# A fused adaLN, cached-attention and gated-MLP decode step: the whole kernel rewritten around one load ring and transposed keys

## The chip, the cores and the metric

The kernel runs on one NeuronCore of a Trainium2 chip. The core has TensorE (PE; its weight loads are listed as PEld), VectorE (DVE), ScalarE (ACT), GpSimd (POOL) and SyncE (SP); 16 DMA engines move data between HBM and the on-chip SBUF, and TensorE writes its results to PSUM. The metric is device time in microseconds (us) of one execution. Before the change the median of three runs is 456.72 us (456.42 to 456.93).

A TensorE matmul needs two instructions: a weight load (LDWEIGHTS) that puts a tile of up to 128 x 128 into the array, and the MATMUL, which streams the other operand's columns through it and sums over the partitions. "A pair" below is one of each.

## The reference

One decode step of a transformer block for 8 sequences, hidden size 1024, in bf16:

```python
def reference(A_x, A_k_cache, A_v_cache, A_wq, A_wo, B_x, B_W_gate, B_W_up, B_W_down, c, w_mod):
    # attention: B=8, Sq=1, D=1024, Hq=32, Hkv=4, Sk=8192, Dh=128
        q = (x @ wq).reshape(B, Sq, Hq, Dh) ...
        k = jnp.repeat(k_cache, rep, axis=1)          # 8 query heads share a kv head
        scores = jnp.einsum('bhqd,bhkd->bhqk', q, k) * Dh ** (-0.5)
        p = _softmax(scores, axis=-1)
        o = jnp.einsum('bhqk,bhkd->bhqd', p, v)
        return ... o.reshape(B, Sq, Hq * Dh) @ wo
    # MLP: F=3584
        h = relu(x @ W_gate) * (x @ W_up);  return h @ W_down
    mod = (_silu(c) @ w_mod).reshape(8, 6, 1, -1)      # sa, ca, ga, sb, cb, gb
    h = _layernorm(x) * (1 + ca) + sa
    x = x + ga * attention(h)
    h = _layernorm(x) * (1 + cb) + sb
    x = x + gb * mlp(h)
```

Everything is read once: the K and V caches are 67 MB each, w_mod 12.6 MB, wq and wo 8.4 MB each, gate, up and down 7.3 MB each, 186 MB in all.

## The kernel before, in words

Activations are kept transposed: features on the 128 partitions, the 8 sequences in the columns. A weight tile of 128 x 128 is the stationary operand and an activation tile of 8 columns streams through it, so nearly every matmul has 8 columns.

The order of the work is written out per engine by a small planner. `gen_sp`, `gen_act`, `gen_dve` and `gen_pe` list each engine's instructions; a first dry run ranks TensorE's events, and the loads are sorted into the two queues by the rank of the event that frees their buffer. SP issues all weights and K, ACT issues V between its own work (all through line 61). Buffers are fixed: four weight slots (`wslot`), four K slots (`ksl`), three V slots (`vsl`), 16 KB per partition each, and a scratch area `scr`. Weights for the later stages go into K and V slots when these come free.

The stages:

- Start: c and x are loaded as rows, the sigmoid is taken (L305), silu and x are transposed on TensorE (L552, L556).
- Modulation: for each of eight 1.5 MB blocks of w_mod, 48 matmuls into one of two PSUM banks (L569), which DVE adds up in SBUF (L386). The first layernorm runs on 8-partition rows (function `layernorm`), and its result is transposed.
- Queries: four 2 MB blocks of wq, 64 matmuls each (L587), added up by DVE (L405); ACT scales and reorders them (L315).
- Attention, batch by batch: for each of the four kv heads 64 score matmuls (L508), whose stationary operand is a K tile as it lies in SBUF, positions on the partitions. DVE takes the maximum over all 2048 score columns of a batch (L410); two f32 matmuls and small DVE operations turn it into a bias on all partitions (L534, L413, L415, L537, L418); DVE subtracts it (L422), ACT takes the exponential (L324), DVE sums it (L427), two more f32 matmuls finish the sum (L542, L545). The 4 x 64 PV matmuls of a batch (L525) are issued in two halves during the next batch.
- After the last batch: 256 wo matmuls (L612), the residual, x1 turned to rows by f32 matmuls (L494), the second layernorm in rows, its transposition (L487).
- MLP: for each of eight blocks of gate and up 56 matmuls (L634), added up by DVE (L460); relu and product (L463); 224 down matmuls (L651) in four blocks; gate, residual, eight transposes of 128 columns (L660), a copy (L482) and the store.

A K slot is freed by its last score matmul, a V slot by its last PV matmul. The K tile goes into the score matmul like this:

```python
kv = T.ksl[:, kslot, :].rearrange("k (c d) -> k c d", d=Dh)
...
T.S_ps[:, col:col + REP], kv[:, cix, :], T.qT[:, b, REP * p:REP * (p + 1)],
```

Of the kernel before, what the change touches and what calls it, by code (L numbers as in the profile page):

```python
# [5 lines left out]
dt = mybir.dt  # L6
# [5 lines left out]
class _Eng:  # L12

    def __init__(self, K, name):
        self.K = K
        self.name = name
        self.count = 0
        self.e = None
        self.sem = None
        self.muted = True  # L20

    def _live(self):
        return self.K.emit and not self.muted

    def op(self, fn, key=None, sync=True):
        if sync:
            self.count += 1
        if self._live():
            ins = fn(self.e)
            if sync:  # L30
                ins.then_inc(self.sem, 1)
        if key is not None:
            self.mark(key)
        return self.count

    def mark(self, key):
        k = (self.name, key)
        if self.K.emit:
            assert self.K.ev[k] == self.count, (k, self.K.ev[k], self.count)
        else:  # L40
            assert k not in self.K.ev, k
            self.K.ev[k] = self.count

    def wait(self, eng_name, key):
        if self._live():
            val = self.K.ev[(eng_name, key)]
            self.e.wait_ge(self.K.engs[eng_name].sem, val)

    def wait_self(self):
        if self._live() and self.count > 0:  # L50
            self.e.wait_ge(self.sem, self.count)

    def wait_dma(self, sem_name, value):
        if self._live():
            self.e.wait_ge(self.K.dsem[sem_name], value)

    def dma(self, out_ap, in_ap, sem_name):
        c = self.K.dcnt.get(sem_name, 0) + 16
        self.K.dcnt[sem_name] = c
        if self._live():  # L60
            self.e.dma_start(out_ap, in_ap).then_inc(self.K.dsem[sem_name], 16)  # L61
        return c


class _K:
    pass


class _T:
    pass  # L70


DBG = {}


def bass_adaLN_cond__gqa_block_cached__glu_gated_reglu__decode_kernel(
# [20 lines left out]
    assert B == 8 and D == 1024 and Dh == 128 and Hq == 32 and G == 4 and REP == 8  # L97
    assert F % 128 == 0 and w_mod.shape[1] == 6 * D
    assert Sk % 128 == 0
    NCX = Sk // 128  # L100
    NCOL = NCX * G * REP
    assert NCOL <= 2048
    KC = D // 128
    NKC2 = F // 128
    inv_sqrt_dh = float(Dh) ** -0.5
    EPS = 1e-5
    NW = 4
    NV = 3
    NKT = 4

    K = _K()
    K.ev = {}
    K.emit = False
    K.dcnt = {}
    K.pe_rank = None
    K.engs = {nm: _Eng(K, nm) for nm in ("sp", "act", "pool", "dve", "pe")}

    wblocks = []
    for kc in range(KC):
        wblocks.append(("mod", kc, [(lambda r: r[:, 0:6 * D], w_mod[128 * kc:128 * (kc + 1), :])]))  # L120
    for jb in range(KC // 2):
        wblocks.append(("wq", jb, [(lambda r: r[:, 0:2 * HQD].rearrange("p (k n) -> p k n", n=HQD),
                                    A_wq[256 * jb:256 * (jb + 1), :].rearrange("(kc p) n -> p kc n", p=128))]))
    for blk in range(4):
        wblocks.append(("wo", blk, [(lambda r: r[:, 0:KC * 1024].rearrange("p (k n) -> p k n", n=1024),
                                     A_wo[1024 * blk:1024 * (blk + 1), :].rearrange("(hh d) n -> d hh n", d=128))]))
# [5 lines left out]
    while r0 < F:  # L132
        rr = min(1024, F - r0)
        wd_rows.append((r0, rr))
        r0 += rr
# [8 lines left out]
    for n in range(B * G):  # L144
        last_k_user[n % NKT] = n
# [626 lines left out]
```

## Time and profile before

| | |
|---|---|
| median of three runs | 456.72 us (456.42 to 456.93) |
| the profiled execution, first to last instruction | 453.9 us; the runs' median is 2.8 us above that span |
| busy time | PE 183.6 us, DVE 100.9, ACT 22.5, POOL 1.3 |
| moved by DMA | 186.40 MB, 411 GB/s over the span |
| score matmuls (L508) | 2048, 58.3 us busy |
| PV matmuls (L525) | 2048, 60.1 us busy |
| DVE passes over a batch's scores (L410, L422, L427) | 2292, 2291 and 3568 ns each, 8 of each |
| K and V loads | 32 of 2048 KB each, median 29.4 and 18.7 us from issue to landing |

The span is that of one profiled execution; the times are of other executions, and include what lies around the span. Busy time of an engine is the union of its instructions' times. The rows of 40 slices cut the span into stretches of 11.35 us. A group's line names the line of the kernel, engine, operation, output and inputs, shape and count, then busy us and the mean ns of one, then the idle time just before them and what ended it. Matmuls are pipelined, so the mean time of one (168 ns) is much longer than their distance in a stream.

### The profile page before, as it was taken

To read this page: it belongs to the slowest core of one execution; us is meant where nothing else is said; L and a number is where in the kernel's file an instruction comes from. 1 tells how busy PE (TensorE), PEld (TensorE's weight loads), DVE (VectorE), ACT (ScalarE), POOL (GpSimd) and SP (SyncE) were. 2 spreads that over 40 slices of the span, in tenths; PEclk is the share of its full clock that TensorE was granted. 3 is DMA by queue.
4 is the path that set the end of the run, shared out by engine and by line. 5 is a ranking of instruction groups with operands and counts; after the bars stand their busy time and mean duration, and the time that the engine had idled before them with its cause. 6 is when DMAs were issued, how large, how long until landed. Compare 5 with 4: busy or idle time off the path is not lost.

```text
span 453.9 us, 11940 instructions
## 1 busy us (share of the span) xinstructions
PE 183.6 (40%) x5784; PEld 170.6 (38%) x5784; DVE 100.9 (22%) x120; ACT 22.5 (5%) x16; POOL 1.3 (0%) x9
## 2 busy tenths in 40 slices
PE   1212433418445226072407240733073573364655
PEld 1212433307345226062406240633063462263655
DVE  5000200062322320043004300430043043003321
ACT  3000001010100100001000100100010011000000
POOL 1000000000000000000000000000000000000000
PEclk9999999999999999999999999999999999999555
DMA  7999999999999999999999999999999989999992
GB/s 309 431 431 426 422 435 428 429 430 372 427 429 424 435 422 425 422 433 422 430 423 430 431 416 430 430 428 419 436 424 432 394 357 428 420 423 424 414 405 77
DMA packets 21662, 186.40 MB, mean 411 GB/s; under 512 B 1624, under 2 KB 1624, under 8 KB 11376
## 3 DMA queue, kind: packets, MB, share of 16 engines
q1 hardware_dynamic: 17008, 118.54, 62.5%
q10 hardware_dynamic: 4608, 67.11, 34.8%
q8 instruction: 45, 0.74, 0.6%
q14 instruction: 1, 0.01, 0.0%
HBM read 185.63 MB, written 0.02 MB: 409 GB/s over the span
## 4 chain that ended last, share of the span: by engine, by line
DMA 65%; PE 19%; DVE 6%; issue 5%; another core or an unknown queue 3%; ACT 1%; SPq 1%
DMA ksl<-in_A_k_cache_dram 43%; DMA vsl<-in_A_v_cache_dram 12%; DMA wslot<-in_w_mod_dram 10%; PE S_ps L508 7%; PE OT_ps L525 4%; PE X_ps L612 2%; DVE guacc L427 2%; PE X_ps L634 1%; PE OT_ps L634 1%; DVE scr L422 1%; PE X_ps L651 1%; ACT scr L324 1%; PE S_ps L494 1%; SPq L61 1%
## 5 line engine op out<-in xcount | busy, mean ns | idle before, releaser
L525 PE MATMUL OT_ps<-scr,vsl 128*128 128x8 bf16 x2048 | 60.1, 168 | 87.5 <-DMA vsl<-in_A_v_cache_dram 76.7
L508 PE MATMUL S_ps<-qT,ksl 128*128 128x8 bf16 x2048 | 58.3, 168 | 89.5 <-DMA ksl<-in_A_k_cache_dram 76.5
L525 PEld LDWEIGHTS OT_ps<-scr,vsl 128*128 128x128 bf16 x2048 | 57.3, 104 | 89.8 <-DMA vsl<-in_A_v_cache_dram 77.8
L508 PEld LDWEIGHTS S_ps<-qT,ksl 128*128 128x128 bf16 x2048 | 56.5, 104 | 91.2 <-DMA ksl<-in_A_k_cache_dram 74.1
L410 DVE TENSOR_REDUCE guacc<-S_ps 128x32 f32<-128x2048 f32 x8 | 18.3, 2292 | 145.5 <-PE S_ps L508 145.5
L427 DVE TENSOR_REDUCE guacc<-scr 128x32 f32<-128x2048 bf16 x8 | 28.5, 3568 | 15.8 <-ACT scr L324 15.8
L324 ACT ACTIVATE scr<-scr 128x2048 bf16<-128x2048 f32 x8 | 15.3, 1909 | 286.4 <-DVE scr L422 286.4
L422 DVE TENSOR_TENSOR scr<-S_ps,guacc 128x2048 f32<-128x2048 f32 x8 | 18.3, 2291 | 0.3
L569 PE MATMUL X_ps<-siluT,wslot 128*128 128x8 bf16 x192 | 5.8, 168 | 17.4 <-DMA wslot<-in_w_mod_dram 17.4
L569 PE MATMUL OT_ps<-siluT,wslot 128*128 128x8 bf16 x192 | 5.8, 168 | 16.5 <-DMA wslot<-in_w_mod_dram 16.5
L569 PEld LDWEIGHTS X_ps<-siluT,wslot 128*128 128x128 bf16 x192 | 5.4, 104 | 17.7 <-DMA wslot<-in_w_mod_dram 15.0
L569 PEld LDWEIGHTS OT_ps<-siluT,wslot 128*128 128x128 bf16 x192 | 5.4, 104 | 16.8 <-DMA wslot<-in_w_mod_dram 16.8
L430 DVE RECIPROCAL guacc<-X_ps 1x32 f32<-1x32 f32 x8 | 2.8, 346 | 37.5 <-PE X_ps L542 37.5
L612 PE MATMUL X_ps<-ot_sb,wslot 128*128 128x8 bf16 x256 | 7.3, 168 | 4.2 <-issue 3.5
L612 PEld LDWEIGHTS X_ps<-ot_sb,wslot 128*128 128x128 bf16 x256 | 7.1, 104 | 4.4 <-issue 3.6
L413 DVE TENSOR_REDUCE guacc<-X_ps 32x1 f32<-32x128 f32 x8 | 2.2, 278 | 22.9 <-PE X_ps L534 22.9
L537 PEld LDWEIGHTS X_ps<-guacc,ones 32*128 32x128 f32 x16 | 4.0, 306 | 8.7 <-DVE guacc L415 8.7
L537 PE MATMUL X_ps<-guacc,ones 32*128 32x32 f32 x16 | 5.0, 406 | 5.1 <-DVE guacc L415 5.1
L386 DVE TENSOR_TENSOR modT<-OT_ps,modT 128x384 f32<-128x384 f32 x4 | 2.2, 558 | 19.5 <-PE OT_ps L569 19.5
L545 PE MATMUL X_ps<-guacc,ones 1*128 1x32 f32 x16 | 5.0, 406 | 3.5 <-DVE guacc L430 3.5
L587 PE MATMUL X_ps<-hT,wslot 128*128 128x8 bf16 x128 | 3.7, 168 | 6.2 <-DMA wslot<-in_A_wq_dram 6.2
L587 PE MATMUL OT_ps<-hT,wslot 128*128 128x8 bf16 x128 | 3.7, 168 | 6.0 <-DMA wslot<-in_A_wq_dram 6.0
(88 smaller groups left out, 107.3 us busy)
## 6 DMA issues: line engine op xcount, KB each, us to landing
vsl<-in_A_v_cache_dram ACTq DMA_DIRECT2D x32, 2048.0 KB, 18.7
ksl<-in_A_k_cache_dram SPq DMA_DIRECT2D x32, 2048.0 KB, 29.4
wslot<-in_w_mod_dram SPq DMA_DIRECT2D x8, 1536.0 KB, 22.5
wslot<-in_A_wq_dram SPq DMA_DIRECT2D x4, 2048.0 KB, 17.0
wslot<-in_A_wo_dram SPq DMA_DIRECT2D x4, 2048.0 KB, 38.5
wslot<-in_B_W_down_dram SPq DMA_DIRECT2D x3, 2048.0 KB, 20.3
ksl<-in_B_W_gate_dram SPq DMA_DIRECT2D x4, 896.0 KB, 23.8
ksl<-in_B_W_up_dram SPq DMA_DIRECT2D x4, 896.0 KB, 25.5
```

What stands on the lines that cost most here:

```text
L324: act.op(lambda e: e.activation(T.pt[:, b % 2, 0:NCOL], T.ssub[:, 0:NCOL], ACT.Exp), key=("exp", b))
L410: dve.op(lambda e: e.tensor_reduce(T.mpart[:, :], T.S_ps[:, 0:NCOL].rearrange("p (c j) -> p j c", c=NCX), AX.X, ALU.max), key=("mpart", b))
L422: dve.op(lambda e: e.tensor_tensor(out=T.ssub[:, 0:NCOL].rearrange("p (c j) -> p c j", c=NCX), in0=T.S_ps[:, 0:NCOL].rearrange("p (c j) -> ...
L427: dve.op(lambda e, b=b: e.tensor_reduce(T.lpart[:, :], T.pt[:, b % 2, 0:NCOL].rearrange("p (c j) -> p j c", c=NCX), AX.X, ALU.add), key=(" ...
L508: pe.op(lambda e, b=b, p=p, kv=kv, cix=cix, col=col: e.matmul(T.S_ps[:, col:col + REP], kv[:, cix, :], T.qT[:, b, REP * p:REP * (p + 1)], ...
L525: pe.op(lambda e, p=p, cix=cix, col=col, vv=vv, ptv=ptv: e.matmul(T.OT_ps[:, col:col + REP], vv[:, cix, :], ptv[:, cix, REP * p:REP * (p + ...
L537: pe.op(lambda e: e.matmul(T.X_ps[:, 128:160], T.ones[0:32, 0:128], T.diag[0:32, 0:32], start=True, stop=True), key=("P2", b))
L545: pe.op(lambda e: e.matmul(T.X_ps[:, 192:224], T.ones[0:1, 0:128], T.rrow[0:1, 0:32], start=True, stop=True), key=("P4", b))
L569: pe.op(lambda e, fb=fb, pb=pb, reg=reg, kc=kc: e.matmul(pb[:, fb * B:fb * B + B], reg[:, 128 * fb:128 * (fb + 1)], T.siluT[:, kc, :], sta ...
L587: pe.op(lambda e, hq=hq, kk=kk, pb=pb, reg3=reg3, jb=jb: e.matmul(pb[:, hq * B:hq * B + B], reg3[:, kk, 128 * hq:128 * (hq + 1)], T.hT[:, ...
L612: pe.op(lambda e, fb=fb, hq=hq, wvs=wvs: e.matmul(T.X_ps[:, fb * B:fb * B + B], wvs[hq // 8][:, hq % 8, 128 * fb:128 * (fb + 1)], T.ot_sb[ ...
L634: pe.op(lambda e, fb=fb, pb=pb, reg=reg, kc=kc, cbase=cbase, wbase=wbase: e.matmul(pb[:, cbase + fb * B:cbase + fb * B + B], reg[:, wbase ...
```

## The change

The kernel is written anew. What it computes per stage stays, except that the scores now sum over the head dimension, as the reference does; before, a K tile went into the score matmul with its positions on the summed partitions.

- **Waits.** A graph (`_Graph`) records readers and writers of each buffer and derives the semaphore waits.
- **Loads.** All loads of weights, K and V are issued by SP in one list (`stream`), into one ring of 11 x 16 KB per partition; each waits for the last TensorE reader of the blocks that it overwrites. c and x are loaded by ACT's queue. w_mod comes in four blocks instead of eight, gate and up in four blocks each, W_down in five parts of 7, 7, 7, 5 and 2 row tiles. K of step n stands beside V of step n-2 in the list, and wo is loaded in four blocks between them.
- **Modulation and queries** add up in PSUM instead of in SBUF.
- **Norms in columns.** Mean and variance come from two f32 matmuls with a 1/1024 matrix on the transposed x; everything runs on 128 partitions.
- **Attention** goes by steps n = 0 to 31, kv head by kv head and within that batch by batch. A step has 8 slots. In each slot TensorE transposes 8 K tiles into one of three PSUM banks (`slot_transpose`), DVE (even slots) or ACT (odd slots) copies the 128 x 1024 result to SBUF (`slot_evac`), TensorE computes the scores of the slot two before (`slot_scores`) and 8 PV matmuls of step n-2 (`slot_pv`). The softmax of step n-1 is spread over slots 2 to 7; its sums come from 8 matmuls with a matrix of ones (`soft_sum`). wo's matmuls are done per kv head inside the steps.
- **x1 and the last gate** are turned to rows spread over four groups of 32 partitions (`to_rows`).
- **Down projection in rows.** hmT (128 x 8) is the stationary operand and W_down streams through in 256 columns, with four outputs at partitions 0, 32, 64 and 96. Gate, residual and four stores of 256 columns follow, without a transposition.

The diff, cut to its core:

```diff
-        def issue_k(eng, n):
-            b, p = n // G, n % G
-            slot = n % NKT
-            if n - NKT >= 0:
-                eng.wait("pe", ("sdone", n - NKT))
-            eng.dma(T.ksl[:, slot, :], A_k_cache[b, p].rearrange("(k c) d -> k (c d)", k=128), "k%d" % slot)
...
-        def issue_v(eng, n):
-            b, p = n // G, n % G
-            slot = n % NV
-            if n - NV >= 0:
-                eng.wait("pe", ("pvdone", n - NV))
-            eng.dma(T.vsl[:, slot, :], A_v_cache[b, p].rearrange("(k c) d -> k (c d)", k=128), "v%d" % slot)
...
-                kv = T.ksl[:, kslot, :].rearrange("k (c d) -> k c d", d=Dh)
-                for cix in range(NCX):
-                    last = (cix == NCX - 1)
-                    col = cix * (G * REP) + REP * p
-                    pe.op(lambda e, b=b, p=p, kv=kv, cix=cix, col=col: e.matmul(
-                        T.S_ps[:, col:col + REP], kv[:, cix, :], T.qT[:, b, REP * p:REP * (p + 1)],
-                        start=True, stop=True),
-                        sync=last, key=(("sdone", n) if last else None))
...
-                        pe.op(lambda e, fb=fb, kk=kk, wv=wv, pbank=pbank, kc2=kc2: e.matmul(
-                            pbank[:, fb * B:fb * B + B], wv[:, kk, 128 * fb:128 * (fb + 1)], T.hmT[:, kc2 + kk, :],
-                            start=(kk == 0), stop=(kk == nk - 1)), sync=last, key=(("fpart", di) if last else None))
...
+    RING = 11 * 8192
+    NKT = 6
+    NSEM = 24
...
+        for i in range(4):
+            block(("mod", i), 2 * 6 * D, w_mod.rearrange("(p k) n -> p k n", k=KD)[:, 2 * i:2 * i + 2, :], (2, 6 * D))
+        for i in range(4):
+            block(("wq", i), 2 * HQD, A_wq[256 * i:256 * (i + 1), :].rearrange("(k p) n -> p k n", p=128), (2, HQD))
+        att = []
+        for n in range(N):
+            gg, b = n // B, n % B
+            att.append((n, ("k", n), A_k_cache[b, gg].rearrange("(p c) d -> p c d", p=128)))
+            att.append((n + 2, ("v", n), A_v_cache[b, gg].rearrange("(p c) d -> p c d", p=128)))
+        for gg in range(G):
+            att.append((B * gg + 10.5, ("wo", gg), A_wo[1024 * gg:1024 * (gg + 1), :].rearrange("(h d) n -> d h n", d=128)))
+        att.sort(key=lambda a: a[0])
+        for _, key, src in att:
+            block(key, 8192, src, (KD, D) if key[0] == "wo" else (NC, Dh))
+        for i in range(4):
+            for nm_, w in (("gate", B_W_gate), ("up", B_W_up)):
+                block((nm_, i), 2 * F, w[256 * i:256 * (i + 1), :].rearrange("(k p) n -> p k n", p=128), (2, F))
+        wd_parts = [(0, 7), (7, 14), (14, 21), (21, 26), (26, 28)]
+        for i, (a, z) in enumerate(wd_parts):
+            block(("wd", i), (z - a) * D, B_W_down[128 * a:128 * z, :].rearrange("(k p) n -> p k n", p=128), (z - a, D))
...
+        def layernorm(src, key):
+
+            flat = lambda t: t[:].rearrange("p k b -> p (k b)")
+            mm(X[:, 0:KD * B], onesD[:], flat(src), True, True, [key, "onesD"], [pX])
+            dve("tensor_reduce", stat[:, 0, :], X[:, 0:KD * B].rearrange("p (k b) -> p b k", b=B), AX.X, ALU.add, reads=[pX], writes=["stat0"])
+            dve("tensor_tensor", out=xcT[:], in0=src[:], in1=bc(stat[:, 0, :], KD), op=ALU.subtract, reads=[key, "stat0"], writes=["xcT"])
+            dve("tensor_tensor", out=tmpT[:], in0=xcT[:], in1=xcT[:], op=ALU.mult, reads=["xcT"], writes=["tmpT"])
...
+        def to_rows(dst, dkey, src, skey):
+            dve("memset", X[:, 0:256], 0.0, writes=[pX])
+            for q in range(4):
+                for j in range(2):
+                    mm(X[32 * q:32 * q + B, 128 * j:128 * (j + 1)], src[:, 2 * q + j, :], identf[:], True, True, [skey, "identf"], [pX])
+            dve("tensor_copy", dst[:], X[:, 0:256], reads=[pX], writes=[dkey])
...
+        def slot_transpose(n, j):
+            t = (8 * n + j) % 3
+            for i in range(8):
+                tr(TB(t)[:, 128 * i:128 * (i + 1)], place[("k", n)][:, 8 * j + i, :], identb[:], ["identb"], [pT[t]], ("k", n))
+
+        def slot_evac(n, j):
+            t, r = (8 * n + j) % 3, (8 * n + j) % NKT
+            if j % 2 == 0:
+                dve("tensor_copy", KT[:, r, :], TB(t), reads=[pT[t]], writes=[("KT", r)])
+            else:
+                act(KT[:, r, :], TB(t), ACT.Copy, reads=[pT[t]], writes=[("KT", r)])
+
+        def slot_scores(G_):
+            n, j = G_ // 8, G_ % 8
+            gg, b = n // B, n % B
+            r = G_ % NKT
+            for i in range(8):
+                cc = 8 * j + i
+                mm(S(n % 2)[:, REP * cc:REP * (cc + 1)], KT[:, r, 128 * i:128 * (i + 1)], qT[:, b, REP * gg:REP * (gg + 1)],
+                   True, True, [("KT", r), "qT"], [pS[n % 2]])
+
+        def slot_pv(n, j):
+            o = O(n % 2)[:, 0:REP]
+            for i in range(8):
+                cc = 8 * j + i
+                mm(o, place[("v", n)][:, cc, :], pt[:, n % 2, REP * cc:REP * (cc + 1)], cc == 0, cc == NC - 1,
+                   [("pt", n % 2)], [pO[n % 2]], ("v", n))
...
+        def soft_max(n):
+            dve("tensor_reduce", mp[:], S(n % 2).rearrange("p (c r) -> p r c", r=REP), AX.X, ALU.max, reads=[pS[n % 2]], writes=["mp"])
+
+        def soft_max_t(n):
+            tr(X[0:8, 0:128], mp[:], identf[:], ["mp", "identf"], [pX])
+
+        def soft_diag(n):
+            dve("tensor_reduce", nm[:], X[0:8, 0:128], AX.X, ALU.max, negate=True, reads=[pX], writes=["nm"])
+            dve("tensor_scalar", out=dg[:], in0=identf[0:8, 0:8], scalar1=nm[:], scalar2=None, op0=ALU.mult, reads=["nm", "identf"], writes=["dg"])
+
+        def soft_bc(n):
+            mm(X[:, 128:128 + REP], ones1[:], dg[:], True, True, ["ones1", "dg"], [pX])
+
+        def soft_sub(n):
+            dve("tensor_copy", nb[:], X[:, 128:128 + REP], reads=[pX], writes=["nb"])
+            dve("tensor_tensor", out=ssub[:].rearrange("p (c r) -> p c r", r=REP), in0=S(n % 2).rearrange("p (c r) -> p c r", r=REP),
+                in1=nb[:, None, :].to_broadcast([128, NC, REP]), op=ALU.add, reads=[pS[n % 2], "nb"], writes=["ssub"])
+
+        def soft_exp(n):
+            act(pt[:, n % 2, :], ssub[:], ACT.Exp, scale=SCALE, reads=["ssub"], writes=[("pt", n % 2)])
+
+        def soft_sum(n):
+            for i in range(8):
+                mm(O(n % 2)[:, 64:128], onesb[:], pt[:, n % 2, 64 * i:64 * (i + 1)], i == 0, i == 7, ["onesb", ("pt", n % 2)], [pO[n % 2]])
...
+        for n in range(N + 4):
+            wg = (n - 11) // B if n >= 11 and (n - 11) % B == 0 else None
+            if n == N + 3:
+                wg = G - 1
+            wbank = (n - 1) % 2
+            for j in range(8):
+                if n < N:
+                    slot_transpose(n, j)
+                    slot_evac(n, j)
+                if 0 <= 8 * n + j - 2 < 8 * N:
+                    slot_scores(8 * n + j - 2)
+                if 0 <= n - 2 < N:
+                    slot_pv(n - 2, j)
+                if j == 0 and 0 <= n - 3 < N:
+                    o_evac(n - 3)
+                if wg is not None and 2 <= j <= 5:
+                    wo_part(wg, wbank, 2 * (j - 2), 2 * (j - 1))
+                if wg is not None and j == 6:
+                    wo_add(wg, wbank)
+                if 0 <= n - 1 < N:
+                    if j == 2:
+                        soft_max(n - 1)
+                    elif j == 3:
+                        soft_max_t(n - 1)
+                    elif j == 4:
+                        soft_diag(n - 1)
+                        soft_bc(n - 1)
+                    elif j == 5:
+                        soft_sub(n - 1)
+                    elif j == 6:
+                        soft_exp(n - 1)
+                    elif j == 7:
+                        soft_sum(n - 1)
...
+        for i, (a, z) in enumerate(wd_parts):
+            for k in range(a, z):
+                for q in range(4):
+                    mm(PS[32 * q:32 * q + B, 2, 0:256], hmT[:, k, :], place[("wd", i)][:, k - a, 256 * q:256 * (q + 1)], k == 0, k == KF - 1,
+                       ["hmT"], [pT[0]], ("wd", i))
+        dve("tensor_tensor", out=fR, in0=PS[:, 2, 0:256], in1=gbR[:], op=ALU.mult, reads=[pT[0], "gbR"], writes=["ssub"])
+        dve("tensor_tensor", out=outR[:], in0=fR, in1=x1R[:], op=ALU.add, reads=["ssub", "x1R"], writes=["outR"])
+        last = []
+        for q in range(4):
+            o = g.dma("sp" if q % 2 == 0 else "act", out.rearrange("b o d -> (b o) d")[:, 256 * q:256 * (q + 1)], outR[32 * q:32 * q + B, :],
+                      osem[q], 16, reads=["outR"])
+            last.append(o)
...
+            o.deps = [users[k] for k in behind[i]]
```

## The prediction, made before the changed kernel was run

> **What bounds the kernel now.** I read the page from the top: busy times, the 40 slices, the queues, the chain of waits; then busy time in chosen stretches, the timeline where TensorE stalls, and the groups that keep shapes apart.
>
> ```profile
> span 453.9 us, 11940 instructions
> ...
> PE 183.6 (40%) x5784; PEld 170.6 (38%) x5784; DVE 100.9 (22%) x120; ACT 22.5 (5%) x16; POOL 1.3 (0%) x9
> ...
> PEclk9999999999999999999999999999999999999555
> DMA  7999999999999999999999999999999989999992
> GB/s 309 431 431 426 422 435 428 429 430 372 427 429 424 435 422 425 422 433 422 430 423 430 431 416 430 430 428 419 436 424 432 394 357 428 420 423 424 414 405 77
> ...
> q8 instruction: 45, 0.74, 0.6%
> ...
> DMA 65%; PE 19%; DVE 6%; issue 5%; another core or an unknown queue 3%; ACT 1%; SPq 1%
> ```
>
> The DMA row is at 9 nearly throughout: the 186.40 MB of loads set the time, no engine is above 40%. Two stretches fall short, and after the last load comes a tail:
>
> ```profile
> 105.00:110.00 5.00, 4.87 (x183) 4.80 (x181) 0.00 (x0) 0.00 (x0) 0.00 (x0) 1.00 0.82 295
> 355.00:370.00 15.00, 8.37 (x264) 7.66 (x263) 2.80 (x3) 0.00 (x0) 0.00 (x0) 1.00 0.86 350
> ...
> 445.00:454.00 9.00, 3.99 (x115) 3.55 (x112) 1.80 (x6) 0.00 (x0) 0.00 (x0) 0.50 0.06 19
> ```
>
> (Columns: stretch, length, busy of PE, weight loads, DVE, ACT, POOL, clock, DMA share, GB/s.) Loads end near 445; 9 us follow.
>
> Next, TensorE when nothing but instructions is missing (timeline):
>
> ```profile
> 111.05 1.63 PE L525 MATMUL OT_ps<-scr,vsl 128*128 128x8 bf16 x56
> ...
> 115.32 2.08 PE L525 MATMUL OT_ps<-scr,vsl 128*128 128x8 bf16 x72 [2.63 <-issue]
> ...
> 121.63 0.51 PE L525 MATMUL OT_ps<-scr,vsl 128*128 128x8 bf16 x13 [0.94 <-issue]
> ```
>
> It resumes at 109.1 (after a short stop), 115.3 and 121.6: a dense stream stops every 6.2-6.3 us. The instruction queue brought 45 packets for 2 x 5784 PE instructions, 257 each, so 128 pairs of weight load and matmul cost at least 6.25 us here, though they run in 3.5. In the gate/up stage the resumes (430.41, 436.37, 442.23) are 5.9 apart.
>
> Last, the clock. The record's 1.00 before 416.5 is no measurement:
>
> ```profile
> L494 PE MATMUL S_ps<-identf,x1T 128*8 128x128 f32 x13 | 2.9, 418 | 0.6 <-DVE x1T L443 0.6
> ...
> L494 PE MATMUL S_ps<-identf,x1T 128*8 128x128 f32 x2 | 0.5, 314 | 0.0
> ...
> L508 PE MATMUL S_ps<-qT,ksl 128*128 128x8 bf16 x2048 | 58.3, 168 | 89.5 <-DMA ksl<-in_A_k_cache_dram 76.5 <-issue 12.8
> L651 PE MATMUL X_ps<-hmT,wslot 128*128 128x8 bf16 x128 | 4.0, 168 | 3.7 <-issue 2.5 <-DVE hmT L463 1.1
> ```
>
> (Line, operation, count | busy us, mean ns.) The first row is 413.3-416.0, the second 416.6-416.8. L508 in the stretch marked 1.00 lasts 168 ns, exactly as L651 after 420, where 0.50 is on record. One f32 stream speeds up as the record begins at 416.5. So this kernel ran at half clock all along; 3 us of back-to-back 128-column f32 passes lifted it for one 3.4 us window, and dense streams of 8-column matmuls (8.5 us from 104.0) never did.
>
> **Loads, one ring on one queue.** Bytes and shapes per row stay, w_mod aside. The stretches 2-52 and 400-445 us run on SP's queue alone, at 418 and 409 GB/s, so one queue suffices. c and x move to ACT's queue, so weights are issued 0.8 us sooner (SP's row has them at 1.51 after two issues; now 0.7). Every load waits only for the last reader of the block eleven ahead, five steps of 10 us before it is needed. The two dips go: 5(1-295/425) + 15(1-350/425) = 1.5 + 2.6 = 4.1 us. About 2,100 more pairs add 16 instruction packets of 16 KB over 16 engines: 0.6 us. Loads end at 445 - 0.8 - 4.1 + 0.6 = 441.
>
> **Attention on TensorE.** Per step (one kv head, one batch) there are now 64 transposes of K, 64 score and 64 PV matmuls, 8 of ones for the sums, two small f32, and 64 wo pairs every 8 steps: 212 pairs against some 128 before. Data per step: (8 x 4.19 + 2.10)/8 = 4.46 MB, at 426 GB/s 10.5 us. An 8-column pair costs 27 ns (L508: 64 in 1.87 us, less 0.17, over 63). A transpose streams 128 columns. The bounds are 27 ns (an 8-column pair) and 213 (an L494 instruction: 3.41 us/16). [...] I take 107 at half clock and 53 at full.
>
> At full clock a step is 8 x (8 x 53 + 16 x 27) = 6.8, sums 0.25, f32 transpose 0.2, broadcast 0.1, wo 0.2, and one stall: soft_bc in slot 4 waits for dg, behind that slot's eviction on DVE: 0.68 (L482, the same copy on 8 partitions) + 0.28 (L413) + 0.23 (L415) + 0.3 handovers, less 0.43 of scores and PV: 1.1. Sum 8.7 us. At half clock: 8 x (8 x 107 + 432 ns) = 10.3, sums 0.43, transpose 0.43, broadcast 0.23, wo 0.2, stall 1.1: 12.6 us. Instruction refill: 212 x 6.25/128 = 10.4.
>
> TensorE may run late: gate and up take 14.7 MB, 35 us, to load, and their 448 pairs at 6/128 us take 21, so 14 us of lateness vanish there, and the ring holds those loads meanwhile. A step of up to 10.5 + 14/33 = 10.9 costs nothing; each 0.1 above costs 3.3 us.
>
> I take the full-clock case. At half clock the transposes fill 6.8 of 12.6 us and other streams raise this to 65-70%; an 8-column stream fills 8/32 at most and didn't lift the clock, f32 passes at about 90% of a window did, so 70% lies nearer the end that did. Even alternating, a step of (8.7 + 12.6)/2 = 10.65 stays free.
>
> Evictions: four on DVE at 0.68 (up to 1.21, L343) and four on ACT at 1.02 (L305; from 0.95, half of L324) per step. DVE in all: 2.7 + max 0.6 + subtract 0.6 + small ones 1.2 = 5.1; ACT 4.1 + 0.65. Both are below 10.5, and scores use a copy two slots (1.7 us or more) old. ACT's copies need no table load between the exps: L315, the same function, brought none. The old 2.3-3.6 us DVE passes were hidden behind loads already and give nothing; nor do the DVE adds of w_mod and wq partial sums, now made in PSUM: TensorE waits for those blocks' loads (7 us each for w_mod) before and after.
>
> **Norms and tail.** The first norm lies under w_mod's loads. The second (columns: two f32 matmuls, ten small DVE operations at 0.2, about 4 us, against 416.8-422.7 before) and the x1 rows (16 f32 instructions, 3.4 us) lie under gate/up loads: nothing. After the last load, today's 9 us are a refill stop, 96 matmuls, DVE, transposes, copy, store (1.8). After: eight 8x256 matmuls of the two-tile block, 256 columns at half clock being 213 ns each, 0.5 us if the four column groups run together, 1.7 in turn, plus up to 4 of backlog; two DVE operations of 0.43 (L405); stores 2.3; up to 1.5 of refill. That is 4 to 10; I take 6, as plain 256-column streams should lift the clock.
>
> [...]
>
> **Sum.** 441 + 6 = 447 us of span, against 453.9. The timed median, 456.72, is 2.8 above this profile's span; I carry that over: 450.
>
> **Rivals.**
> *Half clock throughout* (the other sign). If passing data through the array in transpose mode doesn't lift the clock, TensorE becomes the bound: K0 arrives at 56, 32 steps of 12.6 less 5 for the first two (no PV), 8 for the last drain steps: 462; norm and rows 7, gate/up 12-21, down 6-14, end 4: 491-508, taken 500, timed 503. It decides from a step of 11.1 on. For it: this kernel never left half clock but once, and for one window. Against: array-filling streams did lift it. Chance 0.33. [...] No transpose stream in this trace is longer than 1 us, so it can't be judged here.
>
> *Refill or part-time clock.* With a refill cycle of 7 us instead of 6.25, or full clock a quarter of the time, a step takes 11.6: 0.7 x 33 = 23 more, 473. For it: the refill is within 1% of the data step already. Against: one load queue instead of two gave 5.9. Chance 0.12 for 457-490.
>
> *The tail eats it.* Column groups in turn at half clock: five parts at 6 us of work per 4.3 of data end 10-11 us late; with the dips partly kept, 456-457. Chance 0.04.
>
> **Numbers.** Full-clock forecast 0.51, its own range 445 to 456. The 8-in-10 range reaches into the half-clock case: 445 to 508. Within 0.2% (0.9 us, about what this measurement can tell) only the tail rival falls. Faster 0.50, same 0.04, slower 0.46.
>
> **What would show it.** Right: transposes at a pitch of about 53 ns after the first steps with clock 1.0 on record, DMA slices at 420-430 up to 440 us without dips, TensorE idle before transposes ended by ring loads, down matmuls within 2 us of the last load. Wrong: a transpose pitch of 107 ns, GB/s near 355 through the attention, SP waiting on TensorE, gate/up matmuls dense after 460; or idle by "issue" above 1 us in every chunk.

## The result, and the profile after

The changed kernel takes 458.45 us (median, 458.11 to 458.77), the kernel before 456.51 us beside it: ratio 1.0041, 95% interval 1.0033 to 1.0050. The forecast was 450 us, faster; it is 0.4% slower. The profiled execution spans 456.8 us, 2.9 more than before.

From the page of the changed kernel, the rows that answer to those shown of before:

```profile
span 456.8 us, 16982 instructions
...
PE 344.4 (75%) x8008; PEld 329.4 (72%) x8008; DVE 175.1 (38%) x422; ACT 155.1 (34%) x169; POOL 1.5 (0%) x11
...
PEclk9999998899798955985987778867875788855555
DMA  8999999999999999999999999999999999999993
GB/s 347 434 415 421 428 425 429 422 423 425 424 426 426 405 428 423 426 423 423 426 413 421 425 424 425 426 424 417 415 425 421 425 428 384 394 416 418 389 342 123
...
q8 instruction: 62, 1.02, 0.9%
...
DMA 48%; PE 38%; DVE 9%; issue 3%; SPq 1%; ACT 1%; DVEq 0%
```

The two dips (372 and 357 GB/s before) are gone, a smaller one (384) has come near 388 us, the DMA row stays at 9, TensorE has idle time left, and yet the loads end later: the last one lands at 452.81 us, against 447.26 before and 441 forecast. Stretches at the end say more (columns: stretch, length, busy of PE, weight loads, DVE, ACT, POOL, clock, DMA share, GB/s):

```profile
441.00:446.00 5.00, 1.67 (x28) 0.81 (x28) 0.00 (x0) 0.00 (x0) 0.00 (x0) 0.50 1.05 398
446.00:450.00 4.00, 1.65 (x28) 0.81 (x28) 0.00 (x0) 0.00 (x0) 0.00 (x0) 0.50 0.54 208
450.00:453.00 3.00, 1.40 (x28) 0.64 (x28) 0.00 (x0) 0.00 (x0) 0.00 (x0) 0.50 0.28 107
```

From 446 on half of the DMA engines' time is unused. Each load of the ring raises its semaphore 16 times, which I take as once for each of the 16 engines, and these landing events, sorted, show two groups (a V load of the changed kernel late in the attention, us):

```
376.2 376.5 376.5 376.5 376.6 376.6 377.9 380.1 | 385.7 385.8 386.9 387.0 387.0 387.2 387.4 387.6
```

The distance between first and last engine grows from 1.9 us (landings near 50) over 5.0 (near 145) and 9.7 (near 295) to 11.4 (near 376), in steps of some 1.5 us, a step about every 51 us. TensorE's instructions come in packets of 16 KB, 62 of them in all, one about every 6.4 us; 51 us are eight packets. The packets' own lengths repeat with a period of eight as well (from 337 us on: 1018, 1018, 1074, 1067, 1060, 1100, 1098, 1086 ns, then 1016). I read from this (the packets' records name no engine) that each packet holds up one engine by some 1.5 us, that the packets take turns among eight engines, and that of the other eight six stay together. The remaining two fall back by 1.7 and 3.9 us, in steps that follow the seven 8 KB packets of a second instruction queue (q14). A load is done when its slowest engine is: the last one lands on its first eight engines at 446.6 to 446.9 and on its last at 452.81, and TensorE goes on at 452.85. The slower eight set the end; the page's rows are means over both groups. I call this theory F.

Two other lines of the forecast are answered here. The transposes in the timeline (start, length, engine, line, operation):

```profile
200.48 0.61 PE L279 MATMUL PS<-identb,ring 128*128 128x128 bf16 x8
...
203.23 1.04 PE L279 MATMUL PS<-identb,ring 128*128 128x128 bf16 x8
```

Eight at full clock, three us later eight at half clock: the clock goes to and fro, 0.80 on average between 60 and 396 us. And after the last load:

```profile
451.57 1.88 PE L275 MATMUL PS<-ring,hmT 128*8 128x256 bf16 x28 [1.55 <-DMA ring<-in_B_W_down_dram]
...
453.50 0.42 DVE L283 TENSOR_TENSOR ssub<-PS,gbR 128x256 f32<-128x256 f32 x1 [16.35 <-PE PS L275]
...
454.41 0.72 SPq L82 DMA_DIRECT2D out_dram<-outR  x2
```

From the last landing to the end 4.0 us pass, against 6.7 before.

### The profile page after: what moved, and what is told of

Read it like the earlier page. It is cut to its first block, busy times and chain, and to the rows that moved or that the text cites. A ratio compares the mean times of both kernels' runs of the same rounds, so it can differ in the third digit from the quotient of the medians.

```text
span 456.8 us, 16982 instructions
## 1 busy us (share of the span) xinstructions
PE 344.4 (75%) x8008; PEld 329.4 (72%) x8008; DVE 175.1 (38%) x422; ACT 155.1 (34%) x169; POOL 1.5 (0%) x11
## 3 DMA queue, kind: packets, MB, share of 16 engines
q8 instruction: 62, 1.02, 0.9%
## 4 chain that ended last, share of the span: by engine, by line
DMA 48%; PE 38%; DVE 9%; issue 3%; SPq 1%; ACT 1%; DVEq 0%
DMA ring<-in_A_k_cache_dram 29%; PE PS L279 22%; PE PS L275 16%; DMA ring<-in_A_wq_dram 9%; DMA ring<-in_B_W_up_dram 6%; DVE KT L283 4%; DMA ring<-in_B_W_down_dram 4%; DVE mp L283 3%; DVE dg L283 1%; DVE nm L283 1%; SPq L507 1%; ACT KT L286 0%; DVE ssub L283 0%; ACT pt L286 0%; DVE rl L283 0%
## 5 line engine op out<-in xcount | busy, mean ns | idle before, releaser
L279 PE MATMUL PS<-identb,ring 128*128 128x128 bf16 x2048 | 193.5, 251 | 11.7 <-DMA ring<-in_A_k_cache_dram 11.1
L286 ACT ACTIVATE KT<-PS 128x1024 bf16<-128x1024 bf16 x128 | 131.1, 1024 | 190.1 <-PE PS L279 140.8
L279 PEld LDWEIGHTS PS<-identb,ring 128*128 128x128 bf16 x2048 | 148.5, 113 | 14.6 <-DMA ring<-in_A_k_cache_dram 12.5
L283 DVE COPY KT<-PS 128x1024 bf16<-128x1024 bf16 x128 | 88.6, 692 | 154.2 <-PE PS L279 152.5
L275 PE MATMUL PS<-qT,KT 128*128 128x8 bf16 x2048 | 93.2, 169 | 0.1
L275 PE MATMUL PS<-pt,ring 128*128 128x8 bf16 x2048 | 87.6, 167 | 2.1 <-issue 2.1
L275 PEld LDWEIGHTS PS<-qT,KT 128*128 128x128 bf16 x2048 | 87.7, 103 | 0.2 <-ACT KT L286 0.2
L275 PEld LDWEIGHTS PS<-pt,ring 128*128 128x128 bf16 x2048 | 70.7, 99 | 2.5 <-issue 2.5
L275 PE MATMUL PS<-dg,ones 8*128 8x8 f32 x64 | 13.9, 287 | 24.9 <-DVE dg L283 24.9
L275 PEld LDWEIGHTS PS<-dg,ones 8*128 8x128 f32 x64 | 10.9, 213 | 27.8 <-DVE dg L283 27.7
L283 DVE TENSOR_TENSOR ssub<-PS,nb 128x512 f32<-128x512 f32 x32 | 22.1, 692 | 1.2
L275 PE MATMUL PS<-siluT,ring 128*128 128x8 bf16 x384 | 10.9, 168 | 14.7 <-DMA ring<-in_w_mod_dram 14.7
L283 DVE TENSOR_REDUCE mp<-PS 128x8 f32<-128x512 f32 x32 | 21.8, 681 | 0.4 <-PE PS L275 0.4
```

Source lines behind the costliest of these rows:

```text
L275: return pe(lambda e: e.matmul(out_, lhsT, rhs, start=start, stop=stop, skip_group_check=True), reads, writes, block, deps)
L279: return pe(lambda e: e.matmul(out_, in_, ident, start=True, stop=True, is_transpose=True), reads, writes, block)
L283: return g.op("dve", lambda e: getattr(e, name)(*args, **kw), reads, writes)
L286: return g.op("act", lambda e: e.activation(*args, **kw), reads, writes)
```

## The experiments

All times are medians; the kernel before took 456.3 to 457.0 beside them. A second finding of the comparison is tested with theory F: DMA packets were a little longer in the changed kernel. Its ring is the first thing in SBUF and starts 128 bytes past a multiple of 2048; the kernel before pads its first load buffer to a multiple of 2048 (`padA`).

**Fewer TensorE instructions.**

```diff
         def slot_pv(n, j):
+            if j != 0:
+                return
-    ... cc == 0, cc == NC - 1,
+    ... cc == 0, cc == 7,
```

> Leaves out 56 of the 64 PV matmuls of each step (so 7/8 of the values), nothing else: 1792 fewer pairs, 14 fewer instruction packets of 16 KB (62 to 48). Theory F (fetch): the end of the loads is set by the eight DMA engines that carry TensorE's instruction packets, and each packet holds up its engine by 1.55 us, so 14/8 x 1.55 = 2.7 us less: 458.45 to 455.7; the spread between the first and the last engine's landing near 375 us goes from 11.4 to about 8.7. Theory T (TensorE's lateness holds up the loads): 56 x 27 to 53 ns = 1.5 to 3 us less per step, so the loads would run unhindered and the time drop to 447. Theory R (small rows and the full SP queue): no change, 458.4.

455.36 us (ratio to before 0.9974, 0.9962 to 0.9985), 3.1 less than the changed kernel.

```profile
span 453.6 us, 13397 instructions
...
q8 instruction: 48, 0.79, 0.7%
```

Of one and the same V load the first engine lands at 356.59 (356.65 in the changed kernel), the last at 365.05 (367.98): only the slower group moved, and the spread fell from 11.3 to 8.5. That is theory F; TensorE's lateness (447 expected) and small rows (458.4) are out. 14/8 packets fewer per engine of that group saved 3.1 us, 1.8 each, a little above the 1.55 expected.

**The ring's start.**

```diff
+        _base = -(-nc.sbuf_base // 32) * 32
+        pad = sb("pad", [128, (-_base % 2048) // 2], bf16)
         ring = sb("ring", [128, RING], bf16)
```

> The ring starts at a multiple of 2048 bytes of a partition, as the first load buffer of the kernel before does; in the changed kernel it starts 128 bytes past one. Theory L (alignment): 16 KB packets go back from 617.5 to 612.5 ns, a K or V load from 4.90 to 4.85 us, 67 loads 2.5 us: 455.9. If the slower packets have another cause: 458.4.

> The kernel before, its first load buffer moved to 128 bytes past a multiple of 2048 (768 bytes of padding in place of 640 short of 2048): where the changed kernel has its ring. Theory L: packets as in the changed kernel (16 KB 617.7 in place of 612.6 ns, 2 KB 88 in place of 84, an instruction packet 1.07 in place of 0.93 us): 4 to 5 us more, 460.5 to 461.5, so that the rewrite without this offset is the faster one. If the offset matters only in the changed kernel: 456.4.

```diff
-        _rem = nc.sbuf_base % 2048
+        _rem = (nc.sbuf_base - 128) % 2048
```

> The changed kernel with its ring 512 bytes past a multiple of 2048 (128 in the changed kernel, 0 in the aligned one). If a multiple of 512 is enough: 453.3 and 611 ns at the 90th percentile of the 16 KB packets; if it takes more: up to 458.4 and 620 ns.

> The same with 256 bytes past a multiple of 2048. If a multiple of 256 is enough: 453.3; if it takes 512: 456 to 458.4.

The last two differ from the aligned one only in the pad, `(512 - _base) % 2048` and `(256 - _base) % 2048` bytes.

Aligned: 453.35 us (ratio 0.9938, 0.9923 to 0.9953), faster than the kernel before. The kernel before with the offset: 460.73 (1.0096, 1.0074 to 1.0119). Ring 512 past: 453.46; 256 past: 453.20. From the trace's DMA records (ns; median and 90th percentile; the fourth column is the sum of the data packets of one engine, a sixteenth of all, those lengthened by over about a tenth counted at the median and the 4-byte ones left out; the last is the mean of an instruction packet):

```
kernel                16 KB        2 KB       sum, us   last landing   instr.
before                611 / 611    84 / 84    437.4     447.26         929
before, 128 past      614 / 620    86 / 93    441.5     451.25         1061
changed (128 past)    613 / 620    85 / 93    440.7     452.81         1069
changed, aligned      611 / 611    84 / 84    437.3     448.39         937
```

The records of one engine overlap a little (between 20 and 440 us 16.1 packets are under way on average), so the sum is some 2 us too large in itself, and only differences between kernels are read from it. At 256 and 512 past, the last landing is at 447.50 and 447.29. The offset costs 3.4 to 4.1 us of data packets and 0.13 us per instruction packet, in both kernels; 256 past (453.20 us) is as good as 0. This term was larger than I had expected of the aligned run (5.1 us instead of 2.5), because I had priced only the 16 KB packets. The 90th percentiles rise by 1.5% (16 KB) and 11% (2 KB), the medians by 0.3 to 0.5% and 1 to 2%; why a start 128 bytes past does this, no run shows.

**Long rows of W_down, and both together.**

```diff
-  B_W_down[128 * a:128 * z, :].rearrange("(k p) n -> p k n", p=128)
+  B_W_down.rearrange("(p k) n -> p k n", k=KF)[:, a:z, :]
...
-  w[:, 128 * f:128 * (f + 1)], h2T
+  w[:, f::KF], h2T
```

> W_down is loaded with 28 neighbouring rows on one partition, so rows of 4 to 14 KB in place of 2 KB; gate and up take every 28th column as their stationary operand, so that hidden unit 28p+k lies on partition p. Theory R (small rows cost, wherever they stand, because every engine is busy to the end): 224 packets of 2 KB per engine at 85 ns become 16 KB-like ones at 76 per 2 KB: 2.0 us less, 456.4. If the last loads are bound by something else than packet time (TensorE late, issue): no change.

> The aligned ring and the long W_down rows together. Theory F says that both shorten the packets of the same engines, so the gains add: 453.35 - 1.4 = 452.0. If either gain was of another kind (a start, a tail), the sum would be 453 or more.

457.07 us alone, 1.4 less; with the aligned ring 452.20 (ratio to before 0.9903, 0.9879 to 0.9927). The gains add within 0.2 us of the 452.0 forecast. This is the fastest version found, 6.2 us below the change as made, 4.4 below the kernel before.

**Dips.**

```diff
-    RING = 11 * 8192
+    RING = 6 * 8192
```

> The changed kernel with a ring of 6 blocks in place of 11. The prediction's step (a dip in the moved bytes is lost time): buffers come free later, dips appear, and each 1% of DMA share lost over the 340 us of attention costs 3.4 us, so 460 to 465. Theory F: what stops first is the eight engines that run ahead; the last engine's landing of each load comes when it did, the spread stays below some 9 us, slices of the moved bytes fall to 400 and less late in the attention, and the time stays at 458.4 within 0.8, as in the kernel before the change.

459.39 us, 0.9 more. GB/s of 40 slices with the short ring:

```profile
GB/s 347 440 412 420 428 427 425 423 426 423 408 393 401 410 427 418 418 424 421 425 398 411 427 407 431 418 423 425 405 430 395 412 425 414 400 416 418 408 387 156
```

Slices of 393 to 405 appear in the attention, and the V load named above lands on its first engine at 365.07 (8.4 us later than with the long ring) and on its last at 368.24 (0.3 later). The fast engines wait for buffers, the page shows it as a dip, and the end moves little; from 4 to 446 us there is no moment with fewer than eight packets under way. The 0.9 us is just outside the 0.8 that theory F allowed and stays open; it is below the 1.6 to 6.6 of the prediction's step.

The dips of the kernel before, from the other side: more matmuls there, then fewer.

```diff
-  for cix in range(NCX):
-      last = (cix == NCX - 1)
+  for rnd, cix in [(r, x) for r in range(2) for x in range(NCX)]:
+      last = (rnd == 1 and cix == NCX - 1)
```

> The kernel before with its 2048 score matmuls made twice (the second time with the same operands and the same result), so 2048 more pairs and 16 more instruction packets, 45 to 61; loads, order and all else stay. The prediction's pricing (16 packets over 16 engines): 0.6 to 1 us more. Theory F (each packet holds up one of eight engines by some 1.45 us in this kernel): 16/8 x 1.45 = 2.9 us more, 459.4. If TensorE's instructions cost the loads nothing: 456.5.

476.62 us, 20 more. That was not a packet's price. Its GB/s, and TensorE in the timeline:

```profile
GB/s 321 427 431 428 423 430 432 425 411 134 396 385 425 432 376 432 429 428 419 427 426 422 423 430 425 426 426 422 431 429 429 300 149 425 428 421 422 418 406 94
```

```profile
154.14 3.56 PE L508 MATMUL S_ps<-qT,ksl 128*128 128x8 bf16 x128 [1.93 <-issue]
...
160.61 3.55 PE L508 MATMUL S_ps<-qT,ksl 128*128 128x8 bf16 x128 [2.92 <-issue]
```

128 pairs every 6.47 us: 192 pairs per step take 9.7 us without the softmax's waits, TensorE fell behind, and at 134 and 149 GB/s all engines waited for buffers: in each of the two dips no packet at all was under way for over 4 us, and the engines idled 7.8 and 10.3 us each on average. With 16/8 x 1.45 more than the 447.26 of before the loads would have ended at 450.2; they ended at 467.05. The run tells nothing of the price of a packet, but shows what a dip that is lost time looks like: the last landings are late too.

```diff
-                for cix in range(NCX):            # pv_pairs
+                for cix in range(NCX // 8):
```

> The kernel before with 8 of the 64 PV matmuls per pair of kv head and batch (7/8 of the values left out): 1792 fewer pairs, 14 fewer instruction packets, and TensorE never late. Theory F: 14/8 x 1.43 = 2.5 us less, 454.0; the dips of the moved bytes at 105 to 112 and 340 to 370 go, and give nothing of their own, since the eight engines that end last never waited. The prediction's step (the dips are lost time): 0.5 us for the packets and 4.1 for the dips, 451.9 or less.

453.50 us (ratio 0.9931, 0.9916 to 0.9946), 2.9 less than before; theory F said 2.5 less, the dips as lost time 4.6.

```profile
GB/s 304 431 430 425 425 429 435 425 431 355 424 434 428 428 434 412 425 431 428 431 421 431 430 422 430 429 429 420 433 426 434 426 389 426 425 424 425 412 390 92
...
q8 instruction: 31, 0.51, 0.4%
```

The second dip shrank (357 to 389), the first stayed. In this one profiled execution the last landing is only 0.8 us earlier (446.44) and the tail 1.2 shorter, so the time fits F and the landing only partly. In the first dip the engines idled 1.1 us each on average, 0.8 in the kernel before; in the second, at least eight packets were always under way, as F has it. Since one dip stayed and the other only shrank, the run is a weak test of what the dips cost.

**TensorE's own pace.**

```diff
+  ... "(p c) d -> p c d", p=128)[:, 0:NC // 2, :]        # K and V loads
+  place[("k", n)][:, (8 * j + i) % (NC // 2), :]
```

> Every K and V load brings only the first half of its block (1.05 MB) and TensorE reads that half twice: the same instructions, half the keys and values left out. Shows TensorE's own pace in the attention, which its loads hid. Start at 53, 33 steps of s, then norm, gate and up dense (448 pairs at 47 ns), down and end, some 38. Prediction's full-clock step of 8.7 us: 378. Refill bound, 212 pairs at 6.25 us per 128 = 10.4 us: 434. Half clock throughout, 12.6: 507. A clock that goes to and fro, 10 to 11: 421 to 454.

416.65 us. Rows of its page:

```profile
PE   1434386999988999899999999898899999897596
...
PEclk9999999588996689768788898968966968968556
DMA  8999999999999857675566577956563567595810
```

This is one execution only. DMA is a third idle (share 0.64 from 150 to 370 us), TensorE at 9: from the third on the exponentials are 9.95 us apart on average, against 10.56 in the changed kernel, where the loads set the pace. That is between the prediction's full-clock 8.7 and the 10.4 of the refill. TensorE was below the 10.9 that cost nothing, but only just below the loads' 10.5. Its longest wait in the changed kernel that is not for loads (us in total, times, longest):

```profile
PE PS L275 <- DVE dg L283: 24.9, 31, 1.0
```

**Loads for the idle half.** The other way to use theory F is to give the unhindered eight more bytes.

```diff
+  for r in range(0, 128, 8):      # wd tiles 21 to 26
+      ins = e.dma_start(place[key][r:r + 8], src[r:r + 8]).then_inc(o.sem, 16)
```

> As the run with long W_down rows, and the 1.31 MB block of it (tiles 21 to 26) is loaded by 16 loads of 8 partitions, each of which uses 8 of the 16 DMA engines. Half of the engines then carry 164 KB of it and the others none, in place of 82 KB each: 3.0 us at 27 GB/s. Theory F (half the engines stand idle for the last 11 us): if the eight are the ones without instruction packets, 3.0 us less than with long rows alone (453.4); if they are the ones with them, or four of each, about 3 us more (459.5), and the landings of these small loads show which. If no engines stand idle at the end: 3 us more in any case.

> As the run before it, and tiles 18 to 26 of W_down (2.10 MB) are issued by GpSimd as 16 loads of 8 partitions, each behind a 256-byte load of 8 partitions that no one uses, so that large and small loads alternate. Theory F: half the engines have nothing left for the last 10 us. If the large ones all fall to those, the other eight have 131 KB less each, 4.9 us at 27 GB/s: 447.1, and first and last engine end together. If they fall to the eight with the instruction packets: 5 us or more above the run before, 457 and up. If each is spread over all sixteen, or goes to the two halves in turn: 452, as the run before.

(The run before the second one is the aligned kernel with long rows, 452.20 us; W_down is cut anew there, so that tiles 18 to 26 are one block.)

```diff
+  for r in range(16):             # GpSimd; wd tiles 18 to 26
+      e.dma_start(small[:, 16 * r:16 * r + 16], c[:, 16 * r:16 * r + 16]).then_inc(ssem, 16)
+      ins = e.dma_start(place[key][8 * r:8 * r + 8], src[8 * r:8 * r + 8]).then_inc(bsem, 16)
```

By the landings the loads of 8 partitions went to the wrong eight: the block before them lands on the first eight engines at 437.2 to 438.7 (437.1 to 438.3 without the edit) and on the others at 450.1 to 452.3 (445.0 to 447.0). 465.44 us, 8.4 more instead of 3: 96 of the 128 pieces (eight for each of the 16 loads) had landed by 450.5, the other 32 came one after the other from 452.3 to 458.3, as two engines with 16 each would bring them. Why these came last stays open.

Issued by GpSimd, alternating with small loads, it became 487.72 us. Rows of its page:

```profile
DMA  8999999999999999999999999999999999999950
GB/s 359 421 424 427 434 424 430 425 428 430 429 427 417 431 428 427 427 426 428 420 429 426 427 426 429 424 419 430 426 428 430 389 421 370 221 207 196 208 206 25
...
q0 software_dynamic: 1024, 2.10, 2.2%
```

From the moment GpSimd issues (404 us) the share stays at 9 and the bytes halve: packets of 7 KB, 272 ns before, have a median of 513 ns between 425 and 435. This edit costs 35 us; the division of the bytes, which was to be tested, cannot be read from it.

**Packets of another engine, and the smallest dose.**

> The aligned kernel with 3584 one-element writes more on GpSimd, which is otherwise idle: 14 more instruction packets of 16 KB, of an engine that no load waits for (the ring gives 3584 columns of 90112 for it). If any engine's instruction packets hold up the eight DMA engines as TensorE's do: 14/8 x 1.45 = 2.5 us more, 455.9. If they go to the other eight, or are fetched in another way: 453.35.

```diff
+        for i in range(3584):
+            pool(lambda e, i=i: e.memset(junk[:, i:i + 1], 0.0))
```

460.84 us, 7.5 more than aligned, three times what F gave.

```profile
POOL 8888888887882000000000000000000000000000
...
GB/s 344 438 411 425 430 427 430 426 423 424 428 428 423 233 312 428 429 430 430 426 427 414 430 428 430 430 423 424 419 432 426 426 426 424 411 423 425 411 379 143
...
q14 instruction: 35, 0.29, 0.2%
```

GpSimd's 28 packets of 8 KB, one each 5 us, all fell on one engine, as the landings of a K load show (us):

```
148.8 148.9 149.0 149.1 149.2 149.8 149.9 151.6 151.7 151.8 151.8 151.9 152.0 152.1 152.3 | 167.9
```

One engine was 16 us late, the ring's buffers ran out, and the other 15 stopped (233 and 312 GB/s from 149 to 172). So what counts is not only the number of packets but how many of them fall on one engine.

```diff
-  for i in range(8):                                        # soft_sum
-      mm(O(n % 2)[:, 64:128], onesb[:], pt[:, n % 2, 64 * i:64 * (i + 1)], ...
+  dve("tensor_reduce", lp[:], pt[:, n % 2, :].rearrange("p (c r) -> p r c", r=REP), ...
+  mm(O(n % 2)[:, 64:64 + REP], onesf[:], lp[:], True, True, ...
```

> The aligned kernel with long W_down rows, and the sums of the softmax made by VectorE (one reduction over the 64 chunks, 0.69 us as for the maximum) with one f32 matmul of 8 columns in place of eight of 64: 192 fewer pairs, 1.5 fewer instruction packets. Theory F: 1.5/8 x 1.45 = 0.27 us less than the run without it, 451.9. VectorE, at 38% of the span, takes 32 x 0.69 us more and delays no load. If the sums on VectorE hold up the evictions: TensorE late, over 452.5.

The sums on VectorE: 452.77 us (452.03 to 454.64), where 0.27 us less than 452.20 was forecast; the last load lands at 446.44, against 446.41. One packet less, no measurable gain.

## Why the prediction was wrong

The forecast was that the loads end at 445 - 0.8 - 4.1 + 0.6 = 441. They ended at 452.81. Point by point:

- **Base, 445.** Read from the fall of GB/s. The last landing was at 447.26: the slower engines were still loading for 2 us. The tail of 9 was too long by the same 2, so this cancels in the sum.
- **Earlier issue, -0.8.** Right: the first w_mod packet starts at 1.8 us, before at 2.5.
- **The dips, -4.1: the step that failed in its mechanism.** Every byte not moved in a dip was priced as lost time. But a load is done when its slowest engine is, and in the second dip it was mostly the other engines that stopped. For 4 us of it the DMA share of the kernel before is one half:

```profile
362.00:366.00 4.00, 3.22 (x121) 3.16 (x119) 2.29 (x1) 0.00 (x0) 0.00 (x0) 1.00 0.50 213
```

By the DMA records at least eight packets were under way in 99% of the time from 361.5 to 366.5. The spread between first and last engine was 12.0 us near 351 and 1.3 after this dip, so those that stopped were those that ran ahead, and the slower eight lost next to nothing. In the first dip (105.6 to 108.5) the engines idled 0.8 us each on average, and the spread stayed (1.9 and 1.7), so there the slower ones waited too. That makes some 0.8 in place of 4.1.
- **Sixteen more packets, +0.6: right in kind, mis-sized.** Seventeen more came. They were spread over 16 engines at their own length (0.6 us as estimated, 1.07 as measured); by the landings they hold up eight engines only, by more than their length. The price of one depends on the run: 1.1 to 1.2 us by the sum for the aligned versions ((448.39 - 437.3 - 1.8) x 8/62 = 1.2; more, if the sum is too large), 1.5 by the steps of the spread, 1.8 by the run with fewer PV matmuls. (The 1.45 used above for the kernel before is what fits its own sum with no waiting at all, 437.4 + 1.7 + 45/8 x 1.45 = 447.3, so it is no independent figure.) 17/8 of a packet at 1.1 to 1.8 is 2.3 to 3.8 us.
- **The ring's start: a term that was missing.** 4.4 us at the last landing (5.3 and 5.5 by the versions at 256 and 512), 5.1 in time; shown in both directions. The change drops the pad (`padA`) ahead of the first load buffer, and the prediction's account of what is removed did not have it. Aligned, the change is 3.0 us faster than the kernel before (453.35 against 456.34), so this term alone turned the sign.

447.26 - 0.7 - 0.8 + (2.3 to 3.8) + (4.4 to 5.5) = 452.5 to 455.1, measured 452.81, near the lower end.

Most of the rest held. Full clock throughout did not: it is 0.80 on average from 60 to 396 us, and TensorE's own step of 9.95 us stayed only 0.5 below the loads' 10.5, so that the attention cost nothing by a small margin. What share of busy time lifts the clock, no run shows; the 8/32 of an 8-column stream was the author's estimate (at 107 ns per 128 columns eight columns are 6.7 of a pair's 27 ns). The 107 and 53 ns of a transpose were the author's choice between 27 and 213, and the run of before does not show them as such; the nearest row there is L660, eight bf16 transposes of 128 columns in 1.01 us at clock 0.50, which is (1010 - 311)/7 = 100 ns each. In the changed kernel transposes go at 0.61 us for eight at full clock (pitch 55, forecast 53) and 1.04 at half (107); evictions 1.02 and 0.69; the stall for dg is 24.9/31 = 0.8 in place of 1.1. TensorE finished the attention at 404.5 and had caught up with gate and up at 416.8. Norms and rows (405 to 411) lay under loads. The tail is 4.0 in place of 6: 28 matmuls of 256 columns take 1.67 us, 60 ns each, where one alone would take 213 by an estimate from the 107 ns for 128 columns, so the four column groups overlap here. The prediction had assumed that these streams would lift the clock; it is 0.50 from 396 us to the end. And what lies around the span was 1.65 us this time, not 2.8: the 2.8 set the median of some executions beside the span of a shorter one. Within one execution the kernel before shows 1.8 to 2.1, the changed one 1.8. From 441 and 6 to 452.81 and 4.0, with 1.15 less around the span, 450 becomes 458.5.

The rivals: half clock throughout fell, since the clock is 1.0, and the pitch 55 ns, in stretches of the attention, the longest 34.1 us (from 85.6 on). Refill as the bound fell: 9.95 us, not 11.6. "The tail eats it" (456 to 457) comes nearest in time, by luck: the tail was shorter than before.

What stays open: the price of an instruction packet, 1.1 to 1.8 us depending on the run, and why it is more than the packet's own length; why the last landing moved by only 0.8 us in the kernel before with fewer PV matmuls; and why two engines came last with the 8-partition loads.

## What to carry to other kernels

Where DMA bounds a kernel, look at when each of the 16 engines lands, not at mean bytes per second. In the kernel before, a dip to half the DMA share over 4 us, in which mostly engines that ran ahead stopped, narrowed the spread from 12.0 to 1.3 us and by this reading cost the latest engine next to nothing. What lengthens the latest engine's list did count, instructions too: 14 of TensorE's packets fewer, by the landings on eight engines only, gave 3.1 us. And try where the load buffers start: the ring at 0, 256 and 512 bytes past a multiple of 2048 took 453.35, 453.20 and 453.46 us, at 128 past 458.45; beside 456.5 for the kernel before, that decided here whether the rewrite was slower or faster.

## What the runs showed of the hardware

- By the landings of the changed kernel, eight of the 16 DMA engines fall behind in steps of some 1.5 us, in turn, as TensorE's instruction packets come (62, one about every 6.4 us); the engines differ by up to 12 us in one stream of loads. GpSimd's 28 packets held up one engine, by 16 us near 150 us.
- With the first load buffer 128 bytes past a multiple of 2048, both kernels had 2 KB packets of 85 or 86 ns in the median and 93 at the 90th percentile in place of 84, 16 KB packets of 613 or 614 and 620 in place of 611, and instruction packets of 1.06 or 1.07 us on average in place of 0.93 or 0.94.
- With GpSimd's own loads of 8 partitions amid SyncE's, the bytes moved fell from 421 to some 210 GB/s for 60 us, while the DMA share stayed at 9 tenths.
- With streams of transposes among 8-column matmuls the clock on record is 0.80 of full over the attention, in stretches of 3 to 34 us at full or half; in the kernel before, the record has one stretch of 3.4 us at full, behind 3 us of f32 matmuls of 128 columns, and half from there to the end.
